# One row maximum in eight taken from a TensorE difference, a ScalarE Relu and a VectorE add-and-maximum

## The chip, the cores and the metric

The kernel runs on one core of one Trainium2 chip. The metric is device time in microseconds (us). Engines are named as the profile names them: PE (TensorE, with PEld for its weight loads), DVE (VectorE), ACT (ScalarE), POOL (GpSimd), SP (SyncE, which issues most DMAs). Every time below is from the kernel's timed runs or from one profiled execution of it.

## The reference

One transformer block on x of 2048 tokens and width 576, all in float32: attention with 32 heads of 18 columns, then a gated feed-forward part of width 4608. Cut to what matters here:

```python
qkv = (_layernorm(x) @ wqkv).reshape(B, S, 3, H, Dh)      # S = 2048, H = 32, Dh = 18
scores = einsum("bhqd,bhkd->bhqk", q, k) * Dh ** -0.5
p = softmax(scores, axis=-1)                              # subtracts each row's maximum
h = x + (einsum("bhqk,bhkd->bhqd", p, v) ...) @ wo
out = h + (gelu(n @ w_gate) * (n @ w_up)) @ w_down        # n = _layernorm(h)
```

The softmax of every head and every query needs the largest of 2048 scores before its exponentials are taken.

## The kernel before

Attention goes by **steps**. A step `n` is a group `g` of 4 heads and a block `qc` of 512 queries; there are 8 groups x 4 blocks = 32 steps. Inside a step the loop runs over 16 **key tiles** `kt` of 128 keys. Q and K are stacks of float16 pieces (high and low parts), 54 rows for one head; heads 0 and 2 of a group lie on rows 0-53, heads 1 and 3 on rows 64-117, so that a pair of matmuls can run on the two halves of the array.

For each key tile the main loop (from L1100 on) writes this work, in this order:

- `scores_pair`, twice: two matmuls (L598) put keys x queries of two heads into one of two PSUM pairs of banks, and one exponential on ScalarE (L600, 128x1024) writes the result to SBUF. The rows' maxima ride as two more rows of the stack, so they must be known a step ahead.
- `take(mxs)`, twice: each call runs the generator of the maxima (`max_unit`) on by one item. An item is two matmuls of 54x512 (L551: 128 queries x 512 keys, two heads) into two banks and two reductions on VectorE (L554), each the largest of 512 along a row into one column of `mx`. A step needs 4 heads x 4 query tiles x 4 key blocks = 64 of them, and the generator runs a step and a half ahead of the scores. The banks are a ring of three (`m_ring = ring(singles[:3])`), which the maxima alone use in the main loop.
- `weigh`: the exponentials of the tile before times V, in float32, into the fourth single bank (L604).

At the end of a step's maxima `max_finish` reduces `mx` once more (L565), and GpSimd and DMAs carry the result into the Q stacks. At the end of a step's weighting `out_block` copies the sum out of its bank on ScalarE (L618); the next step's `weigh` waits for that copy.

PE, ACT, DVE and POOL execute in the order in which the code is written (`manual_schedule`), so an instruction that waits holds up all behind it on its engine. Ahead of the main loop a prelude interleaves the first maxima with products that are left from before (`fill`); in the last three steps the output projection and the split of the feed-forward weights come in between.

Of the kernel before, what the change touches and what calls it, by code (L numbers as in the profile page):

```python
# [11 lines left out]
F16 = mybir.dt.float16  # L12
F32 = mybir.dt.float32
I32 = mybir.dt.int32
AF = mybir.ActivationFunctionType
ALU = mybir.AluOpType
AX = mybir.AxisListType

P = 128
# [12 lines left out]
def tile_block(  # L32
# [18 lines left out]
    nc = tc.nc  # L51
# [5 lines left out]
    TB = min(512, S)  # L57
    NB = S // TB
# [6 lines left out]
    NG = H // 4  # L65
    R1 = 3 * DH
# [12 lines left out]
    def ring(items):  # L79
        while True:  # L80
            yield from items

    pair_ring = ring(pairs2)
    m_ring = ring(singles)
    

    nat = const.tile([P, NT, D], F32, name="nat")
# [6 lines left out]
    def view(region, off, shape, dtype=None):  # L94

        dtype = dtype or region.dtype
        v = region if dtype == region.dtype else region.bitcast(dtype)
        size = 4 if dtype == F32 else 2
        n = math.prod(shape)
        assert off % size == 0  # L100
        v = v[:, off // size : off // size + n]
        if len(shape) == 2:
            v = v.rearrange("p (a b) -> p a b", b=shape[1])
        elif len(shape) == 3:
            v = v.rearrange("p (a b c) -> p a b c", b=shape[1], c=shape[2])
        return v
# [193 lines left out]
    def run(it):  # L300
        for _ in it:
            pass
# [8 lines left out]
    def take(it, n=1):  # L311
        for _ in range(n):
            next(it, None)
# [93 lines left out]
    def v_block(b):  # L407
        for t in range(b * TPB, (b + 1) * TPB):
            yield from v_rows(t)
# [100 lines left out]
    def stack_set(region):  # L510
        return [[view(region, 2 * S * (2 * pr + i), (S,), F16) for i in range(2)]
                for pr in range(2)]

    def half(j, rows):
        return slice(64 * j, 64 * j + rows)

    sets = [stack_set(A), stack_set(W)]

    def init_set(st):
        for pr in range(2):  # L520
            for j in range(2):
                nc.sync.dma_start(
                    st[pr][1][64 * j + R1 : 64 * j + R1 + 2].rearrange("p (a b) -> p a b", b=256),
                    neg.unsqueeze(1).to_broadcast([2, S // 256, 256]))

    def load_stacks(g):
        st = sets[g % 2]
        for pr in range(2):
            eng = nc.sync if pr == 0 else nc.gpsimd
            Q, K = st[pr]  # L530
            for j in range(2):
                h = 4 * g + 2 * pr + j
                o = 64 * j
                kr = slice(D + h * DH, D + (h + 1) * DH)
                qr = slice(h * DH, (h + 1) * DH)
                for i, (qs, ks) in enumerate(((qk_hi, qk_hi), (qk_hi, qk_lo), (qk_lo, qk_hi))):
                    rows = slice(o + i * DH, o + (i + 1) * DH)
                    eng.dma_start(Q[rows], qs[qr])
                    eng.dma_start(K[rows], ks[kr])

    def max_unit(n, u, mx):

        g, qc = divmod(n, NB)
        t, kc = divmod(u, NB)
        q0 = qc * TB + t * P
        for pr in range(2):
            Q, K = sets[g % 2][pr]
            pms = [next(m_ring) for j in range(2)]
            for j in range(2):
                r = half(j, R1)  # L550
                nc.tensor.matmul(pms[j][:, :TB], Q[r, q0 : q0 + P],  # L551
                                 K[r, kc * TB : (kc + 1) * TB], start=True, stop=True)
            for j in range(2):
                nc.vector.tensor_reduce(mx[:, t, 2 * pr + j, kc : kc + 1], pms[j][:, :TB],  # L554
                                        axis=AX.X, op=ALU.max)
            yield

    mms = [const.tile([P, P], F16, name=f"mm{i}") for i in range(2)]
    for mm in mms:
# [2 lines left out]
    def max_finish(n, mx):  # L562
        g, qc = divmod(n, NB)
        m = small.tile([P, 4, TPB], F32, tag="m", name="m")
        nc.vector.tensor_reduce(m, mx.rearrange("p t h c -> p h t c"), axis=AX.X, op=ALU.max)  # L565
        mm = mms[n % 2]
        hst = mm[:, : 8 * TPB].rearrange("p (h s t) -> p h s t", h=4, s=2)
        nc.gpsimd.tensor_scalar_mul(m, m, 1 / MSC)
        nc.gpsimd.tensor_copy(hst[:, :, 0], m)
        nc.gpsimd.tensor_sub(hst[:, :, 1], m, hst[:, :, 0])  # L570
        mT = small.tile([P, 1, P], F16, tag="mT", name="mT")
        nc.sync.dma_start_transpose(mT, mm)
        for pr in range(2):
            Q = sets[g % 2][pr][0]
            for j in range(2):
                k = (4 * pr + 2 * j) * TPB
                row = 64 * j + R1
                nc.sync.dma_start(Q[row : row + 2, qc * TB : (qc + 1) * TB],
                                  mT[k : k + 2 * TPB, 0])
# [2 lines left out]
    pes = [view(WK, 2 * 4 * TB * i, (2, TB)) for i in range(NPE)]  # L582

    O0 = 4 * (NB - 1) * TPB * D
    nat1 = nat.rearrange("p t d -> p (t d)")
    oTs = [view(nat1, O0 + 4 * TB * i, (TB,)) for i in range(2)]
    rcb = view(nat1, O0 + 8 * TB, (TB,))
    ohl = view(nat1, O0 + 12 * TB, (2, TB), F16)
# [2 lines left out]
    def scores_pair(n, kt, pr):  # L591

        g, qc = divmod(n, NB)
        pS = next(pair_ring)
        Q, K = sets[g % 2][pr]
        for j in range(2):
            r = half(j, R1 + 2)
            nc.tensor.matmul(pS[:, j, :TB], K[r, kt * P : (kt + 1) * P],  # L598
                             Q[r, qc * TB : (qc + 1) * TB], start=True, stop=True)
        nc.scalar.activation(pes[(2 * kt + pr) % NPE], pS[:, :, :TB], AF.Exp, scale=ex_reg)  # L600
# [63 lines left out]
    UPS = TPB * NB  # L664
    AHEAD = UPS + 8 * UPS // 16

    def maxima():

        for n in range(NS):
            mx = small.tile([P, TPB, 4, NB], F32, tag="mx", name="mx")  # L670
            for u in range(UPS):
                yield from max_unit(n, u, mx)
            max_finish(n, mx)

    oh = view(W, 6 * 2 * S, (NK + 1, D))
# [168 lines left out]
    def blank_rows():  # L844
        nc.gpsimd.memset(W8[3 * KR :, 4:, 2], 0.0)
# [222 lines left out]
    def other_products():  # L1068
        for b in range(1, NB):
            yield from v_block(b)  # L1070
        for j in (1, 6, 2, 7, 3, 8):
            for b in range(1, NB):
                yield from qk_tile(j, b, next(pair_ring)[:, 0])
# [4 lines left out]
    def keep(it):  # L1078
        kept.append((yield from it))

    mxs = maxima()
    init_set(sets[0])
    load_stacks(0)
    fill = other_products()
    side = iter(())
    take(fill, 14)
    for _ in range(AHEAD):
        take(mxs, 2)
        take(fill, 3)
    m_ring = ring(singles[:3])  # L1090
    prev = None
    for n in range(NS):
        g, qc = divmod(n, NB)
        acc = singles[3]
        late = n > NS - NB
        for kt in range(NT):
            take(mxs)
            for pr in range(2):
                scores_pair(n, kt, pr)
            take(fill, 2)  # L1100
            take(side, 3 if g == NG - 1 else 1)
            take(mxs)
            if prev is not None:
                weigh(*prev)
                if prev[0] != n:
                    ob = out_block(prev[0], prev[2])
                    next(ob)
            prev = (n, kt, acc)
            if n and kt in ((2 if n == NS - 1 else 3, 6) if late else (2, 4)):
                take(ob)  # L1110
            if late and kt == 11:
                run(fill)
                fill = wo_block(qc - 1, m_ring)
                if qc == 2:
                    rows = rows0()
            if n == NS - 1:
                take(rows, 2)
            if g == 0 and qc == 0 and kt == NT - 1:
                run(fill)
                init_set(sets[1])  # L1120
            if g + 1 < NG and kt == 2 and qc == (1 if g == 0 and NB > 1 else 0):
                load_stacks(g + 1)
            if n == 1 and kt == 8:
                load_w(of, wo, nc.gpsimd)
            if n == 2 and kt == 4:
                side = prepare_wo()
            if n == NS - NB and kt == 2:
                blank_rows()
                load_matrix(w_gate, 0, nc.gpsimd)
            if n == NS - 2 and kt == NT // 2:  # L1130
                by = nc.vector.tensor_scalar_mul
                side = chain(split_matrix(0, 0, by, lambda: load_matrix(w_up, 0, nc.gpsimd), space=6), pause(10),
                             split_matrix(0, 1, by, lambda: load_matrix(w_gate, 1, nc.gpsimd), space=6),
                             pause(10), until_ready(second))
# [16 lines left out]
    m_ring = ring([singles[3], more[3]])  # L1151
# [89 lines left out]
```

## Time and profile before

| | |
|---|---|
| median of 3 runs | 2767.03 us (2765.87 to 2768.52) |
| profiled execution | 2769.64 us, its span 2767.8 us, mean TensorE clock 0.991 |
| reductions of L554 | 2048, from 122.4 to 1454.1 us |
| exponentials of L600 | 1024, from 227.8 to 1539.0 us |
| rest | feed-forward part, to the end |

The groups of the profile are read as: line, engine, operation, output<-input, count, then busy time and the mean length of one in ns, then the idle time of the engine just before them and what ended it. A mean length is not the distance from one instruction to the next: neighbours overlap a little. The timeline gives start, length, engine, line and count, neighbours of one line merged.

### The profile page before, as it was taken

Reading aid. Unit: us, or ns where it says so; the run is one execution under the profiler, and the core shown is the slowest. Engines: PE = TensorE matmul, PEld = TensorE weight load, DVE = VectorE, ACT = ScalarE, POOL = GpSimd, SP = SyncE. Lnnn points to the kernel's source line nnn. Section 1 sums busy time; section 2 is a strip of 40 time slices with the busy share of each in tenths; the row PEclk is TensorE's granted clock in tenths of the full one; section 3 lists DMA queues with packets and bytes.
Section 4 is the critical chain, followed back from the end, with each engine's and each line's share of the span. In section 5 each row is a group of like instructions: output and inputs, shape, how many; then the busy total and the mean of one; then the engine's idle time right before and its main releaser. Section 6 shows DMA issues by size and latency. Waiting matters only on the chain.

```text
span 2767.8 us, 43717 instructions
## 1 busy us (share of the span) xinstructions
PE 2634.6 (95%) x16665; PEld 1092.7 (39%) x16665; DVE 2165.9 (78%) x3890; ACT 1525.3 (55%) x1880; POOL 707.0 (26%) x891
## 2 busy tenths in 40 slices
PE   6999999999999999999997999999999999999999
PEld 2542222222222222222232555555555555555555
DVE  6379999999999999999996767575757575656563
ACT  5216877777777777777765344343434333333332
POOL 2100431122212221221215543232322222322221
PEclk9999999999999999999999999999999999999999
DMA  8311110010101000010113441010101010101011
GB/s 216 85 46 38 48 40 13 17 34 15 37 11 40 15 24 24 14 40 14 23 29 81 94 78 49 11 49 21 40 22 42 20 48 22 39 22 39 22 58 39
DMA packets 162904, 111.99 MB, mean 40 GB/s; under 512 B 82796, under 2 KB 141712, under 8 KB 162694
## 3 DMA queue, kind: packets, MB, share of 16 engines
q1 hardware_dynamic: 154706, 96.13, 12.9%
q0 software_dynamic: 7856, 13.06, 1.8%
q8 instruction: 130, 2.13, 0.3%
q14 instruction: 80, 0.66, 0.1%
q10 hardware_dynamic: 132, 0.01, 0.0%
HBM read 74.45 MB, written 14.42 MB: 32 GB/s over the span
## 4 chain that ended last, share of the span: by engine, by line
PE 49%; DVE 46%; POOL 2%; DMA 1%; issue 1%; ACT 1%; SPq 0%; DVEq 0%; POOLq 0%; ACTq 0%
DVE mx L554 43%; PE more L971 13%; PE bank L971 13%; PE bank L298 10%; PE more L298 8%; PE pair L298 4%; PE bank L551 1%; PE bank L604 1%; DVE st L186 1%; DMA X<-A 0%; DMA A<-qk_hi 0%; DVE W L282 0%; DVE m L565 0%; DVE nat L715 0%; DMA WK<-in_A_x_dram 0%
## 5 line engine op out<-in xcount | busy, mean ns | idle before, releaser
L554 DVE TENSOR_REDUCE mx<-bank 128x1 f32<-128x512 f32 x2048 | 1264.6, 682 | 26.0 <-PE bank L551 26.0
L600 ACT ACTIVATE WK<-pair 128x1024 f32<-128x1024 f32 x1024 | 991.6, 1021 | 298.7 <-PE pair L598 298.4
L604 PE MATMUL bank<-WK,V 128*32 128x512 f32 x4096 | 547.3, 606 | 0.2 <-ACT nat L618 0.2
L298 PEld LDWEIGHTS <-WK 128*128 128x128 f16 x3456 | 338.1, 98 | 91.0 <-POOL WK L985 2.8
L971 PEld LDWEIGHTS <-W 128*128 128x128 f16 x2394 | 234.6, 98 | 284.9 <-issue 8.2
L551 PE MATMUL bank<-W 54*128 54x512 f16 x1024 | 290.8, 381 | 37.7 <-DVE mx L554 7.6
L551 PE MATMUL bank<-A 54*128 54x512 f16 x1024 | 280.0, 381 | 36.9 <-DVE mx L554 7.3
L604 PEld LDWEIGHTS bank<-WK,V 128*32 128x32 f32 x4096 | 81.0, 108 | 438.8 <-issue 412.3
L627 POOL TENSOR_TENSOR rp<-rc,minus_one 128x16 f32<-128x16 f32 x28 | 81.8, 2922 | 612.1 <-DMA rc<-nat 612.1
L298 PE MATMUL more<-W,WK 128*128 128x288 f16 x1728 | 235.4, 286 | 2.5 <-POOL WK L985 2.5
L298 PE MATMUL bank<-W,WK 128*128 128x288 f16 x1728 | 235.2, 286 | 0.0
L971 PE MATMUL bank<-X,W 128*128 128x512 f16 x792 | 223.8, 379 | 0.0
L971 PE MATMUL bank<-V,W 128*128 128x512 f16 x720 | 203.6, 381 | 0.0
L869 POOL TENSOR_TENSOR A<-A 128x384 f32<-128x384 f32 x144 | 145.7, 1032 | 200.4 <-DMA A<-in_B_w_up_dram 134.8
L985 POOL TENSOR_TENSOR WK<-tmp,WK 128x512 f16<-128x512 f32 x73 | 86.8, 1189 | 304.0 <-ACT WK L982 303.6
L598 PE MATMUL pair<-W 56*128 56x512 f16 x1024 | 156.4, 378 | 3.3 <-ACT WK L600 2.6
L551 PEld LDWEIGHTS <-W 54*128 54x128 f16 x1024 | 59.6, 92 | 246.8 <-issue 218.5
L598 PE MATMUL pair<-A 56*128 56x512 f16 x1024 | 153.8, 375 | 0.2
L551 PEld LDWEIGHTS <-A 54*128 54x128 f16 x1024 | 57.2, 93 | 233.8 <-issue 206.0
L989 ACT COPY tmp<-more 128x512 f32<-128x512 f32 x36 | 20.9, 582 | 225.4 <-PE more L971 192.1
L1061 DVE SCALAR_TENSOR_TENSOR nat<-bank,p_dsc,nat 128x288 f32<-128x288 f32 x144 | 74.4, 517 | 89.8 <-PE bank L298 88.1
L885 ACT ACTIVATE W<-A,p_s_m 128x768 f16<-128x768 f32 (+1 forms) x78 | 78.2, 1035 | 119.8 <-DVE p_s_m L171 119.5
(277 smaller groups left out, 2895.6 us busy)
## 6 DMA issues: line engine op xcount, KB each, us to landing
A<-in_B_w_down_dram SPq DMA_DIRECT2D x8, 1152.0 KB
A<-in_B_w_gate_dram SPq DMA_DIRECT2D x64, 128.0 KB
A<-in_B_w_up_dram SPq DMA_DIRECT2D x64, 128.0 KB
nat<-rc SPq DMA_DIRECT2D x31, 256.0 KB
qk_hi<-qk SPq DMA_DIRECT2D x36, 128.0 KB
qk_lo<-qk SPq DMA_DIRECT2D x36, 128.0 KB
out_dram<-nat SPq DMA_DIRECT2D x16, 288.0 KB
X<-nat SPq DMA_DIRECT2D x100, 36.0 KB
```

Of the source, the lines that this page charges most:

```text
L298: nc.tensor.matmul(dst, a, b, start=(i == 0), stop=(i == len(pairs) - 1))
L551: nc.tensor.matmul(pms[j][:, :TB], Q[r, q0 : q0 + P], K[r, kc * TB : (kc + 1) * TB], start=True, stop=True)
L554: nc.vector.tensor_reduce(mx[:, t, 2 * pr + j, kc : kc + 1], pms[j][:, :TB], axis=AX.X, op=ALU.max)
L598: nc.tensor.matmul(pS[:, j, :TB], K[r, kt * P : (kt + 1) * P], Q[r, qc * TB : (qc + 1) * TB], start=True, stop=True)
L600: nc.scalar.activation(pes[(2 * kt + pr) % NPE], pS[:, :, :TB], AF.Exp, scale=ex_reg)
L604: nc.tensor.matmul(acc[32 * hh : 32 * hh + 32, :TB], Vg[n // NB][:, kt * G4 + hh * VC : kt * G4 + hh * VC + 32], pes[(2 * kt + hh // 2) % ...
L627: nc.gpsimd.tensor_tensor(rc, den, minus_one.to_broadcast([P, R]), op=ALU.pow)
L869: op(W8[:, d], W8[:, a], W8[:, b])
L885: by = hi_on or (lambda dst, src, k: nc.scalar.activation(dst, src, AF.Copy, scale=k))
L971: nc.tensor.matmul(bank, w, x_, start=start and i == 0, stop=i == len(mm) - 1, skip_group_check=not start)
L985: nc.gpsimd.tensor_sub(hl[:, 2 * i + j], v, hh[:, 2 * i + j])
L1061: nc.vector.scalar_tensor_tensor(nat[:, t, ws], pt[:, :HALF], dsc, nat[:, t, ws], op0=ALU.mult, op1=ALU.add)
```

## The change

Take a head's two neighbouring key blocks with scores a and b. The largest of both is the largest of max(a, b) = a + max(b - a, 0). The change uses this for head 0 of each group, for key blocks (0, 1) and (2, 3) of every query tile: TensorE makes b - a in one bank, by a matmul with K and a second one with a negated copy of K onto the same bank ("over"); ScalarE writes the positive part to a row in SBUF (Relu); VectorE adds it to the bank of a and takes the largest in the same instruction ("both"). In all 8 of a step's 64 reductions go, and 8 others become the new operation. The other 48 stay. The column of `mx` that is then not written is filled with -3e38 by GpSimd. The first step (n = 0) has no such pairs. GpSimd makes the negated copies, two instructions for each group.

```diff
+    negs = [view(nat1, 12288 + 4 * TB * i, (NB // 2, TB), F16) for i in range(2)]
+    rows_of = ring([view(nat1, 18432 + 4 * TB * i, (TB,)) for i in range(4)])
+    def negate(g):
+        r = half(0, R1)
+        K = sets[g % 2][0][1]
+        for i in range(NB // 2):
+            nc.gpsimd.tensor_scalar_mul(negs[g % 2][r, i], K[r, 2 * i * TB : (2 * i + 1) * TB], -1.0)
+    def max_banks(n, mx, todo):
...
+            nc.tensor.matmul(pm[:, :TB], Q[r, q0 : q0 + P], K[r, kc * TB : (kc + 1) * TB],
+                             start=True, stop=kind != "over")
+            if kind == "over":
+                nc.tensor.matmul(pm[:, :TB], Q[r, q0 : q0 + P], negs[g % 2][r, kc // 2],
+                                 start=False, stop=True)
...
+            if kind == "over":
+                row = next(rows_of)
+                nc.scalar.activation(row, pm[:, :TB], AF.Relu)
+                excess.append(row)
+            elif kind == "both":
+                row = excess.pop(0)
+                nc.vector.tensor_tensor_reduce(row, pm[:, :TB], row, 1.0, LOWEST, ALU.add, ALU.max, dst)
+            else:
+                nc.vector.tensor_reduce(dst, pm[:, :TB], axis=AX.X, op=ALU.max)
...
-            for u in range(UPS):
-                yield from max_unit(n, u, mx)
+            over, both = ("over", "both") if n else ("one", "one")
+            if n:
+                nc.gpsimd.memset(mx[:, :, 0, 1::2], LOWEST)
+            for u in range(0, UPS, 2):
+                t, k = divmod(u, NB)
+                for todo in ((("one", t, k, 2), ("one", t, k, 3)),
+                             (("one", t, k, 1), (over, t, k + 1, 0)),
+                             (("one", t, k + 1, 1),),
+                             (("one", t, k + 1, 2), ("one", t, k + 1, 3)),
+                             ((both, t, k, 0),)):
+                    max_banks(n, mx, todo)
+                    yield
...
-            take(mxs)
-            for pr in range(2):
-                scores_pair(n, kt, pr)
+            if kt % 2:
+                take(mxs, 2)
+                scores_pair(n, kt, 0)
+                scores_pair(n, kt, 1)
+            else:
+                take(mxs, kt + n > 0)
+                scores_pair(n, kt, 0)
+                take(mxs)
+                scores_pair(n, kt, 1)
             take(fill, 2)
             take(side, 3 if g == NG - 1 else 1)
-            take(mxs)
+            if kt % 2:
+                take(mxs)
...
+            if g + 1 < NG and kt == 8 and qc == (1 if g == 0 and NB > 1 else 0):
+                negate(g + 1)
```

Eight maxima (two key blocks, four heads) are now five items, A to E in the order of `todo`: A = heads 2 and 3 of the first block; B = head 1 of the first block and "over" of head 0; C = head 1 of the second block; D = heads 2 and 3 of the second block; E = "both" of head 0. Over two key tiles the main loop places them so: even tile: E, scores, A, scores, weighting; odd tile: B, C, scores, scores, D, weighting.

TensorE at the start of a tile, before: behind the weighting (into bank_69) come two maxima on banks of the ring (66, 67, 68), then the scores.

```order
L604 MATMUL bank_69<-WK,V 32x512 x4
L551 LDWEIGHTS A
L551 MATMUL bank_68<-A 128x512 [waits DVE_49]
L551 LDWEIGHTS A
L551 MATMUL bank_66<-A 128x512 [waits DVE_49]
L598 LDWEIGHTS A
L598 MATMUL pair_73<-A 128x512 [waits Activation_49]
```

TensorE at the start of an odd tile in the change: B's maximum (bank_68), "over" with its two matmuls (bank_66; the negated copy lies in nat), C (bank_67), then the scores.

```order
L626 MATMUL bank_69<-WK,V 32x512 x4
L563 LDWEIGHTS A
L563 MATMUL bank_68<-A 128x512 [waits DVE_49]
L563 LDWEIGHTS A
L563 MATMUL bank_66<-A 128x512 [waits DVE_49]
L566 LDWEIGHTS A
L566 MATMUL bank_66<-nat,A 128x512
L563 LDWEIGHTS A
L563 MATMUL bank_67<-A 128x512 [waits DVE_49]
L620 LDWEIGHTS A
L620 MATMUL pair_73<-A 128x512 [waits Activation_49]
```

Three banks are now taken ahead of the scores, and four matmuls stand there where two stood. At the end of the same tile D takes the next two banks, the second of which is that of "over"; behind the weighting stands E, by itself:

```order
L563 MATMUL bank_68<-A 128x512 [waits DVE_49]
L563 LDWEIGHTS A
L563 MATMUL bank_66<-A 128x512 [waits Activation_49]
L626 MATMUL bank_69<-WK,V 32x512 x4
L563 LDWEIGHTS A
L563 MATMUL bank_67<-A 128x512 [waits DVE_49]
L620 LDWEIGHTS A
L620 MATMUL pair_73<-A 128x512 [waits Activation_49]
```

What moved: D's second matmul, and with it the weighting behind it, now waits for ScalarE where all such matmuls waited for VectorE.

VectorE over E, A, B, C, D in the change (L577 is the new operation, written as two instructions; before, a uniform row of L554 stood here):

```order
L577 ISA nat,mx<-bank_67,nat 128x512 [waits PE_49,Activation_49]
L577 ISA mx 128x1
L579 TENSOR_REDUCE mx<-bank_68 128x1 [waits PE_49]
L579 TENSOR_REDUCE mx<-bank_66 128x1 [waits PE_49]
L579 TENSOR_REDUCE mx<-bank_67 128x1 [waits PE_49]
L579 TENSOR_REDUCE mx<-bank_66 128x1 [waits PE_49]
L579 TENSOR_REDUCE mx<-bank_67 128x1 [waits PE_49]
L579 TENSOR_REDUCE mx<-bank_68 128x1 [waits PE_49]
L577 ISA nat,mx<-bank_66,nat 128x512 [waits PE_49,Activation_49]
```

Seven operations in eight instructions stand where eight reductions stood, and the first of them waits for ScalarE too. On ScalarE a Relu (L573) stands between the two exponentials of an even tile and the two of the odd one.

More of the change, by code (lines that the diff above doesn't have):

```diff
@@ L539, in load_stacks @@
                     eng.dma_start(K[rows], ks[kr])
-    def max_unit(n, u, mx):
-        g, qc = divmod(n, NB)
-        t, kc = divmod(u, NB)
-        q0 = qc * TB + t * P
-        for pr in range(2):
[L547 to L556, printed above, removed]
+    nat1 = nat.rearrange("p t d -> p (t d)")
@@ new lines, in tile_block @@
+    negs = [view(nat1, 12288 + 4 * TB * i, (NB // 2, TB), F16) for i in range(2)]
+    rows_of = ring([view(nat1, 18432 + 4 * TB * i, (TB,)) for i in range(4)])
+    LOWEST = -3.0e38
+    excess = []
+    def negate(g):
[4 more added lines that the diff above has]
+    def max_banks(n, mx, todo):
+        g, qc = divmod(n, NB)
+        pms = []
+        for kind, t, kc, h in todo:
+            Q, K = sets[g % 2][h // 2]
+            q0 = qc * TB + t * P
+            r = half(h % 2, R1)
+            pm = next(m_ring)
+            nc.tensor.matmul(pm[:, :TB], Q[r, q0 : q0 + P], K[r, kc * TB : (kc + 1) * TB],
[3 more added lines that the diff above has]
+                                 start=False, stop=True)
+            pms.append(pm)
+        for (kind, t, kc, h), pm in zip(todo, pms):
+            dst = mx[:, t, h, kc : kc + 1]
+            if kind == "over":
[7 more added lines that the diff above has]
+                nc.vector.tensor_reduce(dst, pm[:, :TB], axis=AX.X, op=ALU.max)
@@ L584, in tile_block @@
     O0 = 4 * (NB - 1) * TPB * D
-    nat1 = nat.rearrange("p t d -> p (t d)")
     oTs = [view(nat1, O0 + 4 * TB * i, (TB,)) for i in range(2)]
@@ L1083, in tile_block @@
     load_stacks(0)
+    negate(0)
     fill = other_products()
@@ L1086, in tile_block @@
     take(fill, 14)
-    for _ in range(AHEAD):
-        take(mxs, 2)
+    for i in range(AHEAD):
+        take(mxs, 2 + i % 2)
         take(fill, 3)
@@ L1096, in tile_block @@
         for kt in range(NT):
-            take(mxs)
-            for pr in range(2):
-                scores_pair(n, kt, pr)
+            if kt % 2:
[7 more added lines that the diff above has]
+                scores_pair(n, kt, 1)
             take(fill, 2)
             take(side, 3 if g == NG - 1 else 1)
-            take(mxs)
+            if kt % 2:
+                take(mxs)
             if prev is not None:
```

## The prediction

> **What bounds the kernel now.** I read the page first: the span, the busy shares, the chain by lines, the costliest groups.
>
> ```profile
> span 2767.8 us, 43717 instructions
> PE 2634.6 (95%) x16665; PEld 1092.7 (39%) x16665; DVE 2165.9 (78%) x3890; ACT 1525.3 (55%) x1880; POOL 707.0 (26%) x891
> DVE mx L554 43%; PE more L971 13%; PE bank L971 13%; PE bank L298 10%; PE more L298 8%; PE pair L298 4%; PE bank L551 1%; PE bank L604 1%; DVE st L186 1%; DMA X<-A 0%; DMA A<-qk_hi 0%; DVE W L282 0%; DVE m L565 0%; DVE nat L715 0%; DMA WK<-in_A_x_dram 0%
> L554 DVE TENSOR_REDUCE mx<-bank 128x1 f32<-128x512 f32 x2048 | 1264.6, 682 | 26.0 <-PE bank L551 26.0
> ```
>
> The chain spends 43% of the span in the row maxima of L554. Then the table by stretches, here two in attention, and the lists by tile and by line that tell how long a step is and where the steps lie.
>
> ```profile
> 1300.00:1400.00 100.00, 94.14 (x646) 20.62 (x648) 99.79 (x166) 79.75 (x85) 22.77 (x31) 1.00 0.10 23
> 1400.00:1500.00 100.00, 93.28 (x682) 34.66 (x674) 76.03 (x151) 63.27 (x68) 31.23 (x58) 0.99 0.18 46
> L565 DVE TENSOR_REDUCE m<-mx x29: 219/219/222, 246.8 to 1361.5; 128x16 f32<-128x64 f32 x29
> L600 ACT ACTIVATE WK<-pair x1024: 1017/1023/1066, 227.8 to 1538.0; 128x1024 f32<-128x1024 f32 x171
> ```
>
> Columns of the first two rows: length, then busy time of PE, PEld, DVE, ACT, POOL, then clock. VectorE is busy 99.8 of 100 us, at clock 1.00, and only past 1400 does other work break in. L565 runs once in a step: 28 steps from 246.8 to 1361.5, 39.8 us each. From the first exponential at 227.8 to about 1382 that is 29 undisturbed steps of the 32.
>
> "Busy" hides what sets the step, so I read single instructions in the timeline of one key tile (kt), TensorE, VectorE and ScalarE:
>
> ```profile
> 1005.91 0.39 PE L551 MATMUL bank<-W 54*128 54x512 f16 x2
> 1006.14 0.60 PE L598 MATMUL pair<-A 56*128 56x512 f16 x4
> 1006.57 0.88 PE L551 MATMUL bank<-W 54*128 54x512 f16 x2
> 1007.08 0.37 PE L551 MATMUL bank<-W 54*128 54x512 f16 x1
> 1007.38 1.06 PE L604 MATMUL bank<-WK,V 128*32 128x512 f32 x8
> 1008.38 0.39 PE L551 MATMUL bank<-W 54*128 54x512 f16 x2
> 1006.33 1.89 DVE L554 TENSOR_REDUCE mx<-bank 128x1 f32<-128x512 f32 x3
> 1006.62 1.94 ACT L600 ACTIVATE WK<-pair 128x1024 f32<-128x1024 f32 x2 [0.77 <-PE pair L598]
> ```
>
> They give every duration of the working below. A matmul on rows 0-53 and one on rows 64-117 start together; the next on the same rows 0.22 later (1005.91, 1006.14; four scores in 0.43). A reduction starts 0.42 after its matmul (1005.91, 1006.33). Three reductions take 1.89, one 0.68, so one follows another after 0.60. The matmul at 1007.08 is the fourth maximum of the tile and waits for the bank of the first: 0.75 after that reduction's start. From it 0.30 to the weighting (1007.38), from there 1.00 to the next matmul (1008.38). An exponential starts 0.48 after its scores; two take 1.94, one 1.02, so they follow after 0.92 and overlap by 0.10. Now the loop closes: 1.00 + 0.42 + 0.75 + 0.30 = **2.47 us per kt**, exactly 1008.38 - 1005.91. It is a chain weighting, matmul, *one* reduction, bank, weighting. The four reductions (2.40) nearly fill it.
>
> **The change, part by part.** In two kt (8 maxima, in the old form 2 x 2.47 = 4.94) the parts E, A, B, C, D of the change put on the engines:
>
> - VectorE: 6 reductions and one add-and-maximum, itself two instructions (main, and the 128x1 read of its result). No row shows this operation. Below: spacing of a reduction plus a tiny operation, 0.60 + 0.07 = 0.67. Nearest: an addition of a PSUM and an SBUF operand of that size, 690 ns against a reduction's 682, so again 0.60 apart, plus the read; ScalarE's read of an accumulator, between 9.24 and 9.34, adds 0.10. I take 0.70. Above: two SBUF operands, 877 ns, or 1031 beside GpSimd, plus a whole 188 ns read: 1.07 and 1.22. Sum: 6 x 0.60 + 0.70 = 4.30.
> - ScalarE: 4 exponentials and one Relu of 128x512 from PSUM. Nearest is the copy of the same shape out of PSUM, 585 ns (less the overlap 0.49); below half an exponential, 0.51; above a gelu, 724. Sum 4 x 0.92 + 0.49 = 4.17.
> - TensorE: one matmul more (the negated block), beside C on the other rows; but E stands alone. 9 places instead of 8; without waits 2 x (1.00 + 0.30) + 7 x 0.22 = 4.14.
>
> ```profile
> L1038 DVE TENSOR_TENSOR WK<-more,WK 128x512 f32<-128x512 f32 x34 | 23.4, 689 | 13.1 <-PE more L971 12.5
> L979 DVE SCALAR_TENSOR_TENSOR A<-tmp,p_hsc,A 128x512 f32<-128x512 f32 x34 | 29.8, 877 | 3.9 <-DVE tmp L1023 0.5
> L754 DVE TENSOR_TENSOR V<-V 128x512 f16<-128x512 f32 x4 | 4.1, 1031 | 0.1
> 358.95 0.15 DVE L691 COPY u_o<-p_u_wo 128x1 f32<-128x1 f32 x1
> 359.02 1.28 DVE L554 TENSOR_REDUCE mx<-bank 128x1 f32<-128x512 f32 x2
> 9.24 0.19 ACT L153 ACTIVATION_READ_ACCUMULATOR A<-WK 128x1 f32 x1
> 9.34 0.67 ACT L153 ACTIVATE A<-WK 128x576 f16<-128x576 f32 x1
> L618 ACT COPY nat<-bank x32: 585/585/586, 268.9 to 1542.8; 128x512 f32<-128x512 f32 x32
> L976 ACT ACTIVATE A<-A,p_gsc 128x512 f32<-128x512 f32 x34 | 24.6, 724 | 0.0
> ```
>
> No engine is full at 4.30, so the length is again a chain, which I walk with 3 banks in a ring (E, A, A, B, over, C, D, D) from E's matmul at 0. Scores 0.22, A 0.44, scores 0.66, weighting 0.96, B and over 1.96, negated block 2.18. VectorE: add-and-maximum 0.42, A 1.12 and 1.72, B 2.38. "Over" needs the bank of the first A: free at 1.12 + 0.75 = 1.87, in time by 0.09. C needs the bank of the second A: 1.72 + 0.75 = 2.47, so C and the scores beside it start then, D's first at 2.38 + 0.75 = 3.13. D's second needs the bank of "over", which ScalarE frees: the exponentials run from 0.70 and 1.62 to 2.54, the Relu starts 0.48 behind the negated block, 2.66, lasts 0.585, and with 0.07 to the release (as 0.75 - 0.68) D's second goes at 3.32. Weighting 3.62, next E **4.62**. The add-and-maximum then starts at 5.04, when VectorE has idled since 4.78.
>
> So the new chain is weighting, negated block, Relu, bank, weighting; 0.32 shorter per two kt. 8 x 4.62 = 36.96 a step. Once a step come two stalls:
>
> - The copy of the weighted sums (0.49 of ScalarE) now stands between the second exponential (2.54) and the Relu: it starts at 3.03, 0.37 late, and D and the weighting with it. Before, that copy lay in ScalarE's idle time (0.77 before the pair shown above).
> - L565 delays A by some 0.23 (39.8 - 16 x 2.47 = 0.28 a step now holds it); "over" has 0.09 of it to spare, 0.14 shows.
>
> Together 37.47 against 39.8, the gain **2.3 us a step, 29 steps: 67 us**.
>
> At nothing: 31 memsets and 16 negations of 54x512 on GpSimd, busy 23 of 100 us, the negations half a step after the load and a step before use (without that cover, about 1 us each); the prelude, where the fill's products set the pace and four negated matmuls add 0.9; the last three steps, where other work sets the pace for much of the time and which return 1 to 2. The rest of the program is not touched. Profiled span: 2767.8 - 67 = 2701; the profiled execution took 2769.64, the median is 2767.03, so the median becomes **2700**.
>
> [...]
>
> **The rivals.**
>
> *Dearer hand-offs.* The chain now has two round trips between TensorE and ScalarE. Priced like the gelu row (724), the Relu sends D's second off 0.14 later: 4.76, x 8 x 29 = 32 us of the gain: 2733. For it: a function, not a copy, and a write to SBUF that the neighbours read. Against it: an exponential of twice the size is 1.02, which leaves about 0.6 for half.
>
> *Half rate: slower.* The operation that adds and reduces could pass each element twice. Price: reductions of 768 and 1152 elements take 948 and 1348, so 1.04 ns an element and 0.15 fixed; twice that for 512 is 1.21.
>
> ```profile
> L127 DVE TENSOR_REDUCE ac_m<-A 128x1 f32<-128x768 f32 x72 | 67.4, 948 | 32.1 <-DMA A<-in_B_w_up_dram 31.7 <-DMA A<-in_B_w_gate_dram 0.2
> L127 DVE TENSOR_REDUCE ac_dn<-A 128x1 f32<-128x1152 f32 x16 | 20.9, 1348 | 12.7 <-DMA A<-in_B_w_down_dram 12.7
> ```
>
> The bank of the first A is late from a price of 0.79 on, and every ns above lengthens the cycle by as much: over, negated block, Relu, D, weighting. At 1.21 the cycle is 5.04; with 0.23 for L565 (the copy is then covered) the step is 40.6, +0.8 x 29 = 23 us: 2790. It decides from a price of 1.08: there the 2.3 us a step are used up. For it speaks that no row shows the operation; against it the 689 ns of L1038, in which a second operand costs no second pass.
> [...] L979 (two SBUF operands, no accumulator) shows 877, not 1.21; no run here shows the operation itself.
>
> *Nothing gained.* If waits that I don't see (the two semaphores before the add-and-maximum, the row handed from ScalarE) cost 0.3 a cycle, the step stays at 39.8: 2767. VectorE's idle 0.26 stands ahead of that operation and covers nearly all of it.
>
> *More.* A Relu of 0.51 gives 4.55: 17 us more, 2683.
>
> **How the numbers follow.** Forecast 0.62 (2700); dearer hand-offs 0.20 (2733); half rate 0.12 (2790); nothing gained 0.03; more 0.03. The forecast's own range is 2683 to 2733, by the bounds of the Relu; the price of the add-and-maximum leaves it alone up to 0.79, and at 1.07 takes back 0.28 x 8 x 29 = 65, to 2765. So 2680 to 2768, which leaves out the half rate. A measurement tells about 0.2% from no change, 5.5 us: faster 0.84, same 0.04, slower 0.12.
>
> **What would show it.** Right: steps between two runs of the max over mx of about 37.5; VectorE idle by 0.2-0.3 ahead of each add-and-maximum, waiting for TensorE; TensorE's second matmul of D waiting for ScalarE; Relu near 585 ns; the two instructions of the add-and-maximum 0.70 together. Wrong: a main instruction over 0.8 (VectorE then idle nowhere), a Relu that starts long after the negated block because exponentials stand ahead of it, or steps of 39 and more with ScalarE busy throughout.

## The result, and the profile after

| | before | the change |
|---|---|---|
| median | 2766.45 us (4 runs) | 2697.57 us (4 runs, 2692.25 to 2699.53) |
| ratio | | 0.9747, 95% interval 0.973 to 0.9764 |
| profiled execution, its span | 2769.64 us, 2767.8 us | 2699.53 us, 2697.5 us |
| forecast | | 2700 us, range 2680 to 2768 |

One of the six runs of the last kernel below, the change again, took 3087.66 us at a granted clock of 0.864 where the others had 0.99; the ranges given leave it out.

The page of the profile after, with its busy shares, the chain by lines and the three groups that took the place of L554:

```profile
span 2697.5 us, 44996 instructions
PE 2628.6 (97%) x16913; PEld 1124.6 (42%) x16913; DVE 2022.2 (75%) x3890; ACT 1651.9 (61%) x2128; POOL 732.6 (27%) x938
PE bank L626 18%; PE more L1003 13%; PE bank L1003 13%; PE bank L563 13%; PE bank L298 11%; PE more L298 8%; PE pair L620 7%; PE pair L298 4%; PE bank L566 2%; ACT WK L622 1%; ACT nat L640 1%; ACT nat L573 1%; DVE st L186 0%; DMA X<-A 0%; DMA A<-qk_hi 0%
L579 DVE TENSOR_REDUCE mx<-bank 128x1 f32<-128x512 f32 x1552 | 965.4, 682 | 31.8 <-PE bank L563 30.9
L577 DVE CUSTOM_DVE_ANT_0 nat<-bank,nat 128x512 f32<-128x512 f32 x248 | 171.4, 691 | 64.2 <-PE pair L620 35.0
L573 ACT ACTIVATE nat<-bank 128x512 f32<-128x512 f32 x248 | 149.1, 601 | 12.8 <-PE bank L566 12.3
```

The reductions, 43% of the chain before, are gone from it. Through attention the chain now runs along TensorE: weighting (L626), maxima (L563), scores (L620), negated block (L566). VectorE now idles ahead of the add-and-maximum (64.2 us ahead of L577). The stretch from 1000 to 1100 us, in the columns of the windows (length, then busy PE, PEld, DVE, ACT, POOL, then clock), says the same in numbers. In the stretch of before that the prediction quotes, VectorE was busy 99.79 us and ScalarE 79.75:

```profile
1000.00:1100.00 100.00, 99.38 (x716) 24.57 (x708) 93.85 (x175) 95.70 (x112) 23.32 (x34) 1.00 0.05 13
```

The lists of single lines and tiles after (shortest, median and longest ns; first and last start):

```profile
L588 DVE TENSOR_REDUCE m<-mx x29: 219/220/222, 249.4 to 1295.0; 128x16 f32<-128x64 f32 x29
L622 ACT ACTIVATE WK<-pair x1024: 1017/1023/1121, 230.6 to 1467.3; 128x1024 f32<-128x1024 f32 x171
L573 ACT ACTIVATE nat<-bank x248: 597/597/657, 190.2 to 1380.5; 128x512 f32<-128x512 f32 x124
```

These rows give the account of the 70.3 us between the spans:

- 28 steps went from 39.81 us each (246.8 to 1361.5 before) to 37.34 (249.4 to 1295.0): 2.47 a step, 71.6 us in the 29 undisturbed ones.
- From the first exponential to the last, attention went from 1310.2 us (227.8 to 1538.0) to 1236.7 (230.6 to 1467.3). That is 73.5 less, so the last three steps give the other 1.9.
- The first exponential starts 2.8 later. In the profiles of the other kernels below it starts between 224.3 and 229.4, and in the second profile of the change itself at 224.8, so 2.8 lies within the spread of single executions.
- What follows the last exponential is as long as before: 1229.8 us, now 1230.2.

-71.6 - 1.9 + 2.8 + 0.4 = -70.3.

The timeline of TensorE after, one cycle of two key tiles (the rows that the working uses):

```profile
1005.16 0.39 PE L563 MATMUL bank<-W 54*128 54x512 f16 x1
1005.17 0.60 PE L620 MATMUL pair<-W 56*128 56x512 f16 x2
1006.13 1.07 PE L626 MATMUL bank<-WK,V 128*32 128x512 f32 x8
1007.13 0.39 PE L563 MATMUL bank<-W 54*128 54x512 f16 x2
1007.36 0.38 PE L566 MATMUL bank<-nat,W 54*128 54x512 f16 x1
1008.30 0.49 PE L563 MATMUL bank<-W 54*128 54x512 f16 x2
1008.72 1.07 PE L626 MATMUL bank<-WK,V 128*32 128x512 f32 x8
1009.72 0.39 PE L563 MATMUL bank<-W 54*128 54x512 f16 x1
```

Of ScalarE:

```profile
1005.88 1.94 ACT L622 ACTIVATE WK<-pair 128x1024 f32<-128x1024 f32 x2 [0.22 <-PE pair L620]
1007.77 0.60 ACT L573 ACTIVATE nat<-bank 128x512 f32<-128x512 f32 x1
1008.34 1.94 ACT L622 ACTIVATE WK<-pair 128x1024 f32<-128x1024 f32 x2
```

And of VectorE:

```profile
1005.69 0.69 DVE L577 CUSTOM_DVE_ANT_0 nat<-bank,nat 128x512 f32<-128x512 f32 x1 [0.21 <-ACT WK L622]
1006.30 0.08 DVE L577 DVE_READ_ACCUMULATOR2_ANT mx<- 128x1 f32 x1
1006.30 3.73 DVE L579 TENSOR_REDUCE mx<-bank 128x1 f32<-128x512 f32 x6
```

From E (1005.16) to the next E (1009.72) the cycle is 4.56 us. Its second half is the chain: weighting 1006.13, 1.00 to B and "over" (1007.13), 0.23 to the negated block (1007.36), 0.41 to the Relu (1007.77), 0.65 to D's second matmul, 0.30 to the weighting (1008.72). D's two matmuls stand in one row: the second ends at 1008.79 and lasts 0.37, so it starts at 1008.42. VectorE idles 0.21 ahead of the add-and-maximum. The row names an exponential as what ended that wait, but the operation starts 0.14 behind the end of E's matmul (1005.16 + 0.39), and that is what it waited for: among 171 of them in 800 us of attention, 170 start 0.52 or 0.53 behind E's start, whether the last exponential had just ended or had ended 0.9 earlier.

### The profile page after: what moved, and what is told of

Same layout as the page of the kernel before. It is cut to its first block, busy times and chain, and to the rows that moved or that the text cites. A ratio compares the mean times of both kernels' runs of the same rounds, so it can differ in the third digit from the quotient of the medians.

```text
span 2697.5 us, 44996 instructions
## 1 busy us (share of the span) xinstructions
PE 2628.6 (97%) x16913; PEld 1124.6 (42%) x16913; DVE 2022.2 (75%) x3890; ACT 1651.9 (61%) x2128; POOL 732.6 (27%) x938
## 4 chain that ended last, share of the span: by engine, by line
PE 90%; DVE 3%; ACT 3%; DMA 2%; issue 2%; POOL 1%; SPq 0%; ACTq 0%; DVEq 0%; POOLq 0%
PE bank L626 18%; PE more L1003 13%; PE bank L1003 13%; PE bank L563 13%; PE bank L298 11%; PE more L298 8%; PE pair L620 7%; PE pair L298 4%; PE bank L566 2%; ACT WK L622 1%; ACT nat L640 1%; ACT nat L573 1%; DVE st L186 0%; DMA X<-A 0%; DMA A<-qk_hi 0%
## 5 line engine op out<-in xcount | busy, mean ns | idle before, releaser
L579 DVE TENSOR_REDUCE mx<-bank 128x1 f32<-128x512 f32 x1552 | 965.4, 682 | 31.8 <-PE bank L563 30.9
L626 PE MATMUL bank<-WK,V 128*32 128x512 f32 x4096 | 547.5, 607 | 0.2 <-ACT nat L640 0.2
L563 PE MATMUL bank<-W 54*128 54x512 f16 x1024 | 272.0, 378 | 4.7 <-ACT nat L573 3.4
L563 PE MATMUL bank<-A 54*128 54x512 f16 x1024 | 263.2, 379 | 7.1 <-DMA A<-qk_hi 3.3
L620 PE MATMUL pair<-A 56*128 56x512 f16 x1024 | 233.6, 380 | 0.9 <-ACT WK L622 0.5
L620 PE MATMUL pair<-W 56*128 56x512 f16 x1024 | 229.7, 382 | 3.2 <-ACT WK L622 2.4
L577 DVE CUSTOM_DVE_ANT_0 nat<-bank,nat 128x512 f32<-128x512 f32 x248 | 171.4, 691 | 64.2 <-PE pair L620 35.0
L563 PEld LDWEIGHTS <-W 54*128 54x128 f16 x1024 | 66.6, 94 | 272.9 <-issue 257.9
L563 PEld LDWEIGHTS <-A 54*128 54x128 f16 x1024 | 63.6, 94 | 257.2 <-issue 241.2
L573 ACT ACTIVATE nat<-bank 128x512 f32<-128x512 f32 x248 | 149.1, 601 | 12.8 <-PE bank L566 12.3
```

What stands on the lines that cost most here:

```text
L563: nc.tensor.matmul(pm[:, :TB], Q[r, q0 : q0 + P], K[r, kc * TB : (kc + 1) * TB], start=True, stop=kind != "over")
L573: nc.scalar.activation(row, pm[:, :TB], AF.Relu)
L577: nc.vector.tensor_tensor_reduce(row, pm[:, :TB], row, 1.0, LOWEST, ALU.add, ALU.max, dst)
L579: nc.vector.tensor_reduce(dst, pm[:, :TB], axis=AX.X, op=ALU.max)
L626: nc.tensor.matmul(acc[32 * hh : 32 * hh + 32, :TB], Vg[n // NB][:, kt * G4 + hh * VC : kt * G4 + hh * VC + 32], pes[(2 * kt + hh // 2) % ...
```

## The experiments

Step lengths in this table are (last - first) / (count - 1) of one row of the lists by tile, the max over `mx` between 330 and 1300 us. For four of the kernels the rows stand below. Cycle lengths, and the shorter lengths of most steps in the text, are differences of single starts of the weighting or of that maximum in the traces. The first four kernels ran beside runs of before of 2765.87 us (median of 7), the last four beside 2769.14 us (11).

| kernel | median us | ratio to before (95%) | cycle | step |
|---|---|---|---|---|
| order alone | 2801.08 | 1.0117 (1.0099 to 1.0136) | 5.08 | 40.8 |
| Relu twice | 2814.49 | 1.0171 (1.0152 to 1.019) | 5.05 | 41.1 |
| nothing added | 2693.82 | 0.9737 (0.972 to 0.9753) | 4.56 | 37.1 |
| copy later | 2695.8 | 0.9741 (0.9723 to 0.976) | 4.56 | 37.2 |
| add-and-maximum twice | 2837.52 | 1.0252 (1.0237 to 1.0267) | 5.19 | 42.0 |
| no negated matmul | 2686.21 | 0.9697 (0.9679 to 0.9715) | 4.50 | 36.8 |
| both stalls moved | 2687.73 | 0.9707 (0.9694 to 0.9719) | 4.56 | 36.9 |
| the change again | 2696.3 | 0.974 (0.9728 to 0.9753) | 4.56 | 37.2 |

**The order alone.** Is the gain one of the new order or of the lighter VectorE? Eight plain reductions stand in the order of the change:

```diff
-            over, both = ("over", "both") if n else ("one", "one")
-            if n:
-                nc.gpsimd.memset(mx[:, :, 0, 1::2], LOWEST)
+            over, both = "one", "one"
```

> The new order of the items alone: in every step all 64 maxima are plain reductions, as the change does it in its first step (no negated matmul, no Relu, no add-and-maximum; everything is computed). My theory (a reduction had to go, since a chain through VectorE sets the pace, and standing E alone costs): eight reductions need 4.80 of a two-tile cycle and E stands by itself behind a weighting, so the cycle is 5.0 to 5.1 us where the old order had 4.94 and the change 4.56: a step of 40.5 to 41.1, 2790 to 2805 us. Rival (the placing of the matmuls, not the lighter VectorE, brought the gain): at or below the 2767 of before.

It came as expected, 2801.08 us. Three views of that kernel follow: its list by tile, VectorE's timeline, and TensorE's.

```profile
L588 DVE TENSOR_REDUCE m<-mx x24: 219/220/221, 332.0 to 1270.5; 128x16 f32<-128x64 f32 x24
```

```profile
1004.94 6.37 DVE L579 TENSOR_REDUCE mx<-bank 128x1 f32<-128x512 f32 x10
```

```profile
1008.30 0.37 PE L563 MATMUL bank<-W 54*128 54x512 f16 x1 [0.22 <-DVE mx L579]
```

The row of VectorE looks like one unbroken run, but it merges neighbours across short pauses. Its ten reductions follow each other after (6.37 - 0.68) / 9 = 0.63 in the mean, against 0.60 without a pause. In single starts, eight at 0.60 take 4.80 of the cycle's 5.08; the other 0.28 is lost ahead of the reductions of B (0.21) and E (0.07), whose matmuls stand right behind a weighting. The windows show the pauses too. VectorE is busy 97.53 of 100 us, where the prediction's stretch of before has 99.79:

```profile
1000.00:1100.00 100.00, 94.87 (x630) 20.40 (x627) 97.53 (x160) 77.52 (x82) 27.07 (x38) 1.00 0.11 30
```

So the pace is a chain through VectorE, not its bare load. In single starts it runs from B's reduction over four more to that of D's second (2.40), from there to A's second matmul, which needs that bank (0.74), to the weighting (0.52), to B (1.00), and to B's reduction (0.42): 5.08. The new order by itself costs 1.0 a step (39.8 to 40.8). Taking one reduction in eight away then brings 3.5, and the change keeps 2.5. So the gain is not one of placement.

**The Relu twice.** If the chain goes through the Relu, a second one lengthens the cycle by its whole length:

```diff
                 nc.scalar.activation(row, pm[:, :TB], AF.Relu)
+                row = next(rows_of)
+                nc.scalar.activation(row, pm[:, :TB], AF.Relu)
```

> ScalarE does each Relu twice, into two rows, and VectorE uses the second; the bank of the difference is free after the second. My theory (the pace is weighting, negated block, Relu, bank, weighting): every ns of ScalarE there lengthens the cycle by as much, 0.5 us: 4.56 to 5.07, a step of 41.2, 2697 to about 2813 us. Rival (an engine's sum sets the pace, VectorE 4.22 or ScalarE 4.2): ScalarE's sum becomes 4 x 0.92 + 2 x 0.52 = 4.72, the cycle at most that: about 2735 us.

ScalarE's timeline of this kernel:

```profile
1014.42 0.63 ACT L573 ACTIVATE nat<-bank 128x512 f32<-128x512 f32 x1
1014.91 0.63 ACT L575 ACTIVATE nat<-bank 128x512 f32<-128x512 f32 x1
```

The second starts 0.49 behind the first, and the cycle grew from 4.56 to 5.05, by 0.49. The median rose by 117 us over the change. 0.49 x 8 x 29 is 114. The rival, a chain on VectorE or TensorE with ScalarE beside it, needed 2735 or less and is out.

**Nothing added.** The add-and-maximum becomes a plain reduction of the same bank, so that it neither reads the row nor waits for ScalarE (its maxima then leave out the positive part):

```diff
-                nc.vector.tensor_tensor_reduce(row, pm[:, :TB], row, 1.0, LOWEST, ALU.add, ALU.max, dst)
+                nc.vector.tensor_reduce(dst, pm[:, :TB], axis=AX.X, op=ALU.max)
```

> The add-and-maximum is replaced by a plain reduction of the same bank; the positive part is made but not added, so the row maximum that softmax subtracts can be too small. My theory: the price of that operation and its wait for ScalarE's row are covered by VectorE's idle time, so the cycle stays at 4.54 to 4.56: 2690 to 2700 us. Rival (the two-semaphore wait and the dearer operation cost what they take, 0.1 us and more a cycle): 2670 us or less.

2693.82 us, and the cycle stays at 4.56 although the costliest new operation is gone. The step is 0.11 shorter, all of it in the cycle that holds the max over `mx` (4.66 where the change has 4.77). The plain reduction also starts earlier, 0.42 behind E's matmul instead of 0.53, and nothing comes of that. Neither the price of the add-and-maximum nor its second wait is on the path.

**The add-and-maximum twice.** From what price on does it decide? It is written twice, the first time into a row that nobody reads:

```diff
+                spare = next(rows_of)
+                nc.vector.tensor_tensor_reduce(spare, pm[:, :TB], row, 1.0, LOWEST, ALU.add, ALU.max, dst)
                 nc.vector.tensor_tensor_reduce(row, pm[:, :TB], row, 1.0, LOWEST, ALU.add, ALU.max, dst)
```

> VectorE does each add-and-maximum twice (the first result to a spare row); the bank of a is free after the second. It measures from which price that operation decides. Its pair of instructions now takes 0.615 us until the next reduction starts. My theory (the bank of the first A, freed 0.745 behind its reduction's start, is wanted by 'over' 1.96 behind E, so the price is covered up to about 0.69 to 0.79 with the 0.53 from E's matmul, and counts in full above): a price of 1.23 gives a cycle of 5.0 to 5.1, a step of 40.5 to 41.1, 2790 to 2810 us. Rival (only VectorE's sum can decide): 6 x 0.60 + 1.23 = 4.83, a step of 39.4, 2760 us.

It was slower than I expected: 2837.52 us. VectorE's timeline of that kernel, and TensorE's with the matmul of "over":

```profile
1006.60 0.69 DVE L578 CUSTOM_DVE_ANT_0 nat<-bank,nat 128x512 f32<-128x512 f32 x1 [0.17 <-PE pair L622]
1007.22 0.08 DVE L578 DVE_READ_ACCUMULATOR2_ANT mx<- 128x1 f32 x1
1007.34 0.69 DVE L579 CUSTOM_DVE_ANT_0 nat<-bank,nat 128x512 f32<-128x512 f32 x1
1007.95 0.09 DVE L579 DVE_READ_ACCUMULATOR2_ANT mx<- 128x1 f32 x1
1007.95 1.88 DVE L581 TENSOR_REDUCE mx<-bank 128x1 f32<-128x512 f32 x3
```

```profile
1008.70 0.37 PE L563 MATMUL bank<-W 54*128 54x512 f16 x1 [0.20 <-DVE mx L581]
```

Two of them are not twice 0.615: the second starts only when the first's read is over (1007.22 + 0.08, then 1007.34, 0.74 behind the first), so the pair costs 1.35 (1006.60 to 1007.95). That was the miss in the expectation. The mechanism is the one that the prediction's second rival describes: the first A is reduced late, its bank comes late, and "over" waits 0.20 for VectorE. VectorE's own sum, 6 x 0.60 + 1.35 = 4.95, is below the measured 5.19, so it is not the bare load. If each ns of price lengthens the cycle by as much, as the prediction has it, the point from which it decides is 1.35 - (5.19 - 4.56) = 0.72. The prediction had 0.79, because its walk starts the operation 0.42 behind E's matmul where 0.53 was measured (0.79 - 0.11 = 0.68); the operation's 0.615 is below all of these.

**No negated matmul.** ScalarE takes the positive part of b alone, so that "over" is one matmul and the chain is shorter by up to 0.23:

```diff
-                             start=True, stop=kind != "over")
-            if kind == "over":
-                nc.tensor.matmul(pm[:, :TB], Q[r, q0 : q0 + P], negs[g % 2][r, kc // 2],
-                                 start=False, stop=True)
+                             start=True, stop=True)
```

> The second matmul of each difference, with the negated block, is left out, so ScalarE takes the positive part of b alone and the row maximum that softmax subtracts can be too large. My theory (that matmul is on the chain but runs beside C, and what it frees is soon taken by the next wait): the Relu can start at most 0.04 earlier, when the exponentials ahead of it end, so the cycle goes from 4.56 to 4.50 or 4.52, 2697 to about 2686 us. Rival (TensorE's load is the bound, each matmul counts): 0.22 a cycle, about 2646 us.

TensorE's and ScalarE's timeline of that kernel, and its list by tile:

```profile
1007.50 1.06 PE L625 MATMUL bank<-WK,V 128*32 128x512 f32 x8
1008.51 0.60 PE L619 MATMUL pair<-W 56*128 56x512 f16 x2
1011.64 0.43 PE L563 MATMUL bank<-W 54*128 54x512 f16 x2
1012.00 0.64 PE L625 MATMUL bank<-WK,V 128*32 128x512 f32 x4
```

```profile
1009.22 1.94 ACT L621 ACTIVATE WK<-pair 128x1024 f32<-128x1024 f32 x2 [0.23 <-PE bank L563]
1011.04 0.60 ACT L572 ACTIVATE nat<-bank 128x512 f32<-128x512 f32 x1
```

```profile
L587 DVE TENSOR_REDUCE m<-mx x26: 219/220/221, 360.2 to 1281.0; 128x16 f32<-128x64 f32 x26
```

As expected, only 0.06 a cycle came of it. The Relu now starts straight behind the two exponentials (1009.22 and 1.82 for two of them is 1011.04). The next chain is this one: weighting 1007.50, 1.01 to the scores, 0.71 to the first exponential, 1.82 for two, then Relu, D's second and weighting with 0.96 together: 4.50. In the change the same queue is 0.07 away: two exponentials from 1005.88 let a Relu start at 1007.70, and it started at 1007.77. Much of the negated block's matmul is thereby covered by ScalarE's queue. The rival is out: were TensorE, busy 99.38 of 100 us in the change, the bound by its load, the missing matmul would have brought 0.22 a cycle.

**The copy later.** The once-a-step copy of the weighted sums goes from before the Relu to behind it:

```diff
             if kt % 2:
                 take(mxs, 2)
+                if kt == 1 and n:
+                    next(ob)
                 scores_pair(n, kt, 0)
...
                 if prev[0] != n:
                     ob = out_block(prev[0], prev[2])
-                    next(ob)
```

> The copy of the weighted sums out of their bank is written behind the Relu of the second key tile of a step, where it stood ahead of it. My theory (in the cycle of 5.01 us that comes once a step, the copy delays the Relu, and with it D and the weighting, by 0.45): the Relu goes at its usual time, the weighting then waits for the copy, some 0.2 us: that cycle falls to about 4.8, the step to 37.0, 2697 to about 2690 us. Rival (the cycle is long for another reason, the scores' wait or the weighting's own bank): 5.01 stays, 2697.

The stall itself, in the timelines of TensorE and of ScalarE of the change:

```profile
1016.48 0.38 PE L566 MATMUL bank<-nat,W 54*128 54x512 f16 x1
1017.99 0.37 PE L563 MATMUL bank<-W 54*128 54x512 f16 x1 [0.20 <-ACT nat L573]
```

```profile
1016.85 0.59 ACT L640 COPY nat<-bank 128x512 f32<-128x512 f32 x1
1017.31 0.63 ACT L573 ACTIVATE nat<-bank 128x512 f32<-128x512 f32 x1
```

From the negated block to the Relu it is 0.83 instead of 0.41, and to D's second matmul 1.51 instead of 1.06: the cycle with the copy takes 5.01, 0.45 more than the others. In this kernel that cycle fell to 4.74. But the copy now delays the exponentials behind it, and the next cycle rose from 4.56 to 4.76, so 0.07 of the 0.45 is left as gain. 2695.8 us cannot be told from the change beside the medians' spread. My expectation was half right: the stall left its place and came up one cycle on.

**Both stalls moved.** The max over `mx` is moved too, from between the last "both" and the next A to behind that item:

```diff
+        late = []
...
                     max_banks(n, mx, todo)
+                    if late:
+                        max_finish(*late.pop())
                     yield
-            max_finish(n, mx)
+            late.append((n, mx))
+        max_finish(*late.pop())
```

> Two moves of what comes once a step: the copy behind the Relu as in late_copy, and the max over mx written behind the next step's first item, so that it no longer stands between the add-and-maximum and the two reductions of A. My theory (that max delays A, and so 'over' and C, in a cycle of 4.77 and the next of 4.62): both of these fall to 4.56 to 4.6, 0.2 us a step; with the copy's 0.07 the step goes from 37.21 to 36.95, 2697 to about 2689 us. Rival (those two cycles are long for another reason, or the max delays D just as much behind A): the step stays at 37.1.

> The changed kernel itself, on the same chip and against the same runs of the kernel before, to compare late_both with: 2692 to 2700 us, a step of 37.21.

The lists by tile, of this kernel and of the change on the same chip:

```profile
L588 DVE TENSOR_REDUCE m<-mx x26: 206/208/211, 363.8 to 1286.1; 128x16 f32<-128x64 f32 x26
```

```profile
L588 DVE TENSOR_REDUCE m<-mx x26: 219/220/222, 359.9 to 1290.8; 128x16 f32<-128x64 f32 x26
```

The steps are 36.89 and 37.24. In the change the two cycles around the max over `mx` take 4.77 and 4.62; here both take 4.56. The median is 2687.73 us (2685.29 to 2689.16) against 2696.3 (2693.81 to 2699.41): 8.6 us less. It beats both the kernel before and the change; only the kernel that leaves the negated matmul out is as fast.

## Why the prediction was right, point by point

- **What bounds it before.** Weighting, max, one reduction, bank, weighting: not tested by itself. In single starts of the trace of before, one reduction in four follows after 0.67 instead of 0.60, so VectorE loses 0.07 a key tile: its load of 2.40 does not close the 2.47, the chain does. The order alone, with 4.80 of 5.08, agrees; the forecast for the new chain, made from the same durations, held.
- **The new chain.** Weighting, negated block, Relu, bank, weighting was forecast, and is what the trace shows, with D's second matmul waiting for ScalarE. The Relu written twice gave its whole 0.49 from start to start to the cycle, and the plain reduction in place of the add-and-maximum gave nothing.
- **The cycle.** 4.62 forecast, 4.56 measured. The term that was off is the 0.48 from the negated block to the Relu, taken from the exponentials. It measured 0.41. The Relu starts 0.03 behind the end of its matmul (1007.36 + 0.38, 1007.77), an exponential 0.11 behind that of its scores (1005.17 + 0.60, 1005.88). Over 8 x 29 cycles this is some 14 us of gain more. (The profile models the ends of matmuls; from start to start the Relu's hand-off is 0.41 and an exponential's about 0.49.)
- **The two stalls.** The copy: 0.37 forecast, 0.45 measured. Behind the copy the Relu starts 3.03 after E's matmul (1014.28 to 1017.31), exactly as in the walk; the stall is longer because the Relu without the copy starts 2.61 behind E instead of 2.66, and behind the copy it lasts 0.63 instead of 0.60. L565 (now L588): 0.14 forecast, 0.27 measured (4.77 + 4.62 - 2 x 4.56). Together they took 0.21 a step back, 6 us.
- **The step.** 37.47 forecast. Most steps measured 37.21 = 8 x 4.56 + 0.45 + 0.27, to rounding. The mean is 37.34, since two steps of the first group, where side work runs beside them, took 38.19 and 39.39; the forecast took the steps as alike.
- **The price of the add-and-maximum.** 0.70 forecast between 0.67 and 1.07 or 1.22. Measured from its start to the next reduction's: 0.61 (1005.69 to 1006.30). That is below the lower bound, because the read of its result takes no time of its own: it starts with the next reduction, at 1006.30. The idle time of 0.2 to 0.3 ahead of it was 0.21. The walk also had the operation start 0.42 behind E's matmul, by the reductions, and it started 0.53 behind. The two errors cancel by luck: the first A is reduced 1.14 behind E (1005.16 to 1006.30), 1.12 in the walk. The upper bound of 877 ns was a mean of two kinds: 27 of the 34 operations took 0.75 us, and seven took 1.22 to 1.61, each beside a TENSOR_TENSOR of GpSimd. The add-and-maximum took 0.69 beside such an instruction as well (49 of the 248).
- **The Relu.** Priced as the copy, 585 ns; it took 597. The rival that priced it like the gelu row (724) did not come.
- **Half rate.** 691 ns a main instruction, where half rate would have been 1.21 us by the prediction's estimate from the reductions of L127. One operand comes from a PSUM bank here (`nat<-bank,nat`); an accumulating operation on two SBUF operands was not run. That a dearer operation there makes the kernel slower, the runs bear out: with the operation doubled, it was slower than before by 2.5%.
- **Nothing gained, more.** The hand-offs to the add-and-maximum stayed under VectorE's idle time, as the plain reduction in its place showed; and the Relu was not shorter than the copy. The cycle that "more" forecast, 4.55, nearly came all the same, by the shorter hand-off and not by a shorter Relu.
- **At nothing.** The last three steps gave 1.9 (1 to 2 forecast). The way to the first exponential took 2.8 more (0.9 forecast). Since two profiles of the change start it at 230.6 and 224.8, the runs neither show nor exclude the 0.9. A negation on GpSimd took 1.48 us (median of the 16); the "about 1 us" was the author's estimate, and the trace shows no wait for one. The feed-forward part did not move.

The median came out 2.4 us below the forecast: the shorter hand-off (-14) was largely balanced by the larger stalls (+6), the two steps with side work (37.34 - 37.21, +4) and the later start in this profile (+2). The chain was right; that its terms, one of them off by 14 us, add up to so near a hit is luck.

## What to carry to other kernels

Here TensorE, VectorE and ScalarE were busy 94.14, 99.79 and 79.75 of 100 us before, and load moved from one to another brought what the loop through their waits became shorter (from 4.94 us to 4.56 for two key tiles), less two stalls once a step. Walk such a loop with start-to-start distances of single instructions, bank by bank, and look at which buffer the new operation hands back and who needs it next. The Relu also waited for what came to stand ahead of it in ScalarE's queue, a copy once a step, which lengthened that cycle by 0.45 us. Moving such a stall is worth a run, but read the next cycle too before counting the gain.

## What the runs showed that I had not expected

- **The read of the result is free.** L577's second instruction (83 ns) starts together with the next reduction, both at 1006.30, so the pair of instructions costs 0.61, hardly more than one plain reduction (0.60). A second add-and-maximum into the same column, however, started only behind the end of the first's read (1007.30, 1007.34): 0.74 behind the first instead of 0.61.
- **It matters which wait comes last.** After its matmul's end, as the profile models it, the Relu starts after 0.03, an exponential after 0.11, an add-and-maximum after 0.14. Each of the three has a second wait, mostly as a semaphore instruction of its own just ahead of it in the queue; the plain reduction in the add-and-maximum's place (0.42 from start to start, not 0.53) has none. The rows of the three, by line:

```profile
L573 ACTq EVENT_SEMAPHORE  x240: 17/17/17, 211.3 to 1374.5; - x120
L622 ACTq EVENT_SEMAPHORE  x1020: 17/17/17, 235.0 to 1466.5; - x170
L577 DVEq EVENT_SEMAPHORE  x245: 21/21/21, 206.0 to 1382.9; - x123
```

  In the cycle above, the Relu's is a wait for VectorE and is over at 1006.35, long before the matmul ends. Those of the exponential (1005.81) and of the add-and-maximum (1005.59) are the waits for TensorE itself, and the operation follows 0.07 and 0.10 behind their start. So in this cycle it is not the number of waits that tells the three apart, but whether the late one stands in an instruction of its own. That this is the whole reason was not tested by a run that swaps the two waits.
- **The second matmul of a pair can start first.** E is written ahead of the scores and starts at 1005.16 on rows 0-53; a score starts at 1005.17, where in the profile of before a matmul on the same rows started 0.23 later (1005.91, 1006.14). So it must be the score written second, on rows 64-117, which has overtaken the first. The trace bears this out: the record at 1005.17 is the one that posts to the exponential, as the second of a pair does, and the one that waits for the free bank, as the first does, starts at 1005.39. The exponential starts only at 1005.88, behind the end of both.
- **A part of the negated matmul is free.** 0.23 us of TensorE in the chain, and 0.06 to be had by leaving it out, since ScalarE's exponentials stand ahead of the Relu anyway.
